# Decode step of two attention and two FFN layers on Trainium2: FFN products moved to other PSUM banks, and pauses between small steps

## The chip, the cores and the metric

The kernel runs on one core of one Trainium2 chip. The metric is the device time of one execution in microseconds (us). The time before is the median of three runs.

## The reference

One token per batch row (8 rows, width D = 640) goes through attention, FFN, attention, FFN. Both attention layers use the same cache of keys and values (32 heads, 4096 positions, 128 wide, in bfloat16) and the same weights; so do both FFNs.

```python
def _A_ref(x, k_cache, v_cache, wq, wo):
    q = (x @ wq).reshape(B, Sq, 32, 128).transpose(0, 2, 1, 3)
    scores = jnp.einsum("bhqd,bhkd->bhqk", q, k_cache) * (128 ** -0.5)
    p = _softmax(scores, axis=-1)
    o = jnp.einsum("bhqk,bhkd->bhqd", p, v_cache)
    return o.transpose(0, 2, 1, 3).reshape(B, Sq, 32 * 128) @ wo

def _B_ref(x, w1, w2):                      # 640 -> 1728 -> 640
    return jnp.maximum(x @ w1, 0) @ w2

x = A_x
x = x + _A_ref(_layernorm(x), A_k_cache, A_v_cache, A_wq, A_wo)
x = x + _B_ref(_layernorm(x), B_w1, B_w2)
x = x + _A_ref(_layernorm(x), A_k_cache, A_v_cache, A_wq, A_wo)
x = x + _B_ref(_layernorm(x), B_w1, B_w2)
```

## The kernel before

**Visits and units.** Work goes by visits. A visit is one pair of heads of one batch row in one layer; there are 2 x 8 x 16 = 256 of them, numbered 0 to 255. A visit has a K part (scores) and a V part (weighted values), and each part has four units of 512 KB, 128 partitions by 4 KB. K48.2 is unit 2 of the K part of visit 48. V parts run one visit behind K parts: K48, K49, V48, V49, K50 and so on. Units are loaded into an arena of 26 slots by DMAs from SyncE (SP, L637). A load takes one to eight units that lie together in memory, if so many neighbouring slots are free.

**Kept tiles.** Since both layers read the same cache, 21 units of each row stay in the arena from the first layer to the second, and three more are parked in PSUM (`stash`, `unstash`). When the first layer of a row ends, 21 slots are held and five are left.

**Turns.** Eight times, once for each row, the first layer of a row ends and its second layer begins. Between the two lie two visits of another layer or row (`AHEAD = 2`); in the second turn these are 48 and 49. In them the FFN of the row that has just ended is computed, then the new mean and variance, and the queries of the second layer. That is the chain that `finish(0, b)` gives: `up` (five groups of matmuls with w1, 15, 15, 15, 15 and 10 of them), `var` and `root` (the layer norm's scale, on GpSimd), `relu`, `down` (five groups of 14 matmuls with w2), `add`, `mean`, `center`, a query Q, `var2`, `root2`, a query Q. The second layer's last row ends with `finish(1, b)`, which does the same for all eight rows at once.

**Small steps of a visit.** After the scores, M1 (maximum, VectorE), T (transpose, PE), M2 (maximum, VectorE), B (broadcast, PE), E (on ScalarE: the negative maximum, then the exponentials), in most visits PT and PC (turn the probabilities), L (their sum, PE) and I (its reciprocal, VectorE); after the values OC (ScalarE empties o_ps), OG, O, W (product with wo) and Y. A query is Q (ten matmuls) and QC (a copy on ScalarE). In most visits ("moving") the cache streams through PE against four columns of weights (L695, L687); around a turn the cache is the weight and the query moves (L705).

**The order.** `plan()` writes out one list of operations for all engines, and that list is the order in which each engine executes. PE takes its instructions in that order. After every unit of products there is a gap. `step()` fills it: each waiting chain offers its next step with a weight (about its number of matmuls), and those are taken until CAP is reached. A step of weight 0 follows at once. `feed()` puts loads into the list when slots come free; it uses a rough clock for the size of a load, which the weights advance.

**PSUM.** Four names matter here. `o_ps` (one bank) takes the values' products, and at a turn the scores of the first of the two visits; `s_ps` (one bank) takes the scores; `small_ps` (one bank) takes nearly every small result, each in columns of its own; `stash_ps` parks units. The FFN's `up` and `down` of one row are in `small_ps` (`ffn_ps`), and the sum L is in `small_ps` (`lsum_ps`), or in `s_ps` (`lsum2_ps`) for both visits before a turn:

```python
lsum2_ps = s_ps[:, 4 * NJ : 6 * NJ]
mean2_ps, var2_ps, q2_ps = (s_ps[:, 6 * NJ + lo : 6 * NJ + hi] for lo, hi in ((0, 1), (1, 2), (2, 4)))
...
h = [ffn_ps[:, :FC].rearrange("p (f b) -> p f b", b=1)] * len(up_parts)
y = ffn_ps[:, FC * B : FC * B + DC].rearrange("p (c b) -> p c b", b=1)
```

Lines that the text names: L549 `up`, L580 `down`, L573 `relu`, L655 queries, L663 their copy, L680, L687 values, L695, L705 scores, L715 M1 at a turn, L739 B, L757 and L761 E, L781 L, L795 OC, L825 W.

Of the kernel before, what the change touches and what calls it, by code (L numbers as in the profile page):

```python
# [12 lines left out]
ALU = mybir.AluOpType  # L13
AX = mybir.AxisListType
# [8 lines left out]
SOON = 4  # L23
PACE, LATE = 0.6, 2
PAD = 2048
AHEAD = 2
BANK = 512
CAP = 20


def tile_at(NP, which, hp):
# [1 line left out]
    return max(0, 2 * hp - 1) if which == "K" else min(2 * hp + 2, 2 * NP - 1)  # L33


def plan(B, NP, n_up, n_down):

# [4 lines left out]
    order1 = list(range(NP - 1, NP - 4, -1)) + list(range(NP - 3))  # L44
    visits = [(0, 0, hp) for hp in order0]
# [11 lines left out]
    moving = [not any(t - AHEAD - 1 <= i < t + 5 for t in turns) and i < NV - 2 for i in range(NV)]  # L57
# [137 lines left out]
    def query(b, n):  # L195

        return [(10, ("Q", b, order1[n])), (0, ("QC", b, order1[n]))]
# [9 lines left out]
    def finish(layer, b):  # L207

        def own(n, *op):
            return n, ("C", layer, b, *op)  # L210

        c = []
        for k in range(n_up):
            c += [own(15, "up", k)]
            if layer:
                c += [own(0, "relu", k)]
            elif k == min(1, n_up - 1):
                c += [own(0, "var"), own(0, "root")]
        if layer:
            for k in range(n_up):  # L220
                c += [own(15, "down", k)] + [own(0, "var"), own(0, "root")] * (k == n_up // 2)
            return c + [own(0, "add")]
        c += [own(0, "relu")] + [own(14, "down", k) for k in range(n_down)] + [own(0, "add")]
        c += [own(2, "mean"), own(0, "center")] + query(b, 0)
        c += [own(1, "var2"), own(0, "root2")] + query(b, 1)
        return c

    feed()
    for which, i in slots:
        layer, b, hp = visits[i]  # L230
        if which == "K":
            if layer == 0 and b == 0 and hp % GP == 0:
                ops.append(("Q0", hp // GP))
                done.add(ops[-1])
            if layer:
                until(("QC", b, hp))
            if i + 2 < NV and visits[i + 2][0] and order1.index(visits[i + 2][2]) > 1:
                chains.append(query(visits[i + 2][1], order1.index(visits[i + 2][2])))
            pad(i)
            if i and (moving[i] or moving[i - 1]):  # L240
                until(("E", i - 1))
            if moving[i] and not moving[i - 1]:
                ops.append(("clear",))
        else:
            until(("PC" if moving[i] else "E", i))
            clock[0] = max(clock[0], ready.pop(i))
        for g in range(UNIT):
            u = find(which, i, g)
            ops.append(("mm", which, i, g, u))
            clock[0] = max(clock[0], lands[u]) + 0.5  # L250
            release(which, i, g)
            if g + 1 < UNIT:
                step()
        if which == "K":
            if layer and hp == order1[0]:
                until(("C", 0, b, "root2"))
            ops.append(("M1", i))
            ready[i] = clock[0] + 3
            step()
            turned = [(4, ("PT", i)), (0, ("PC", i))] if moving[i] else [(1, None)]  # L260
            chains.append([(1, ("T", i)), (0, ("M2", i)), (1, ("B", i)), (0, ("E", i))] + turned + [(1, ("L", i)), (0, ("I", i))])
        else:
            until(("I", i))
            if i + 1 < NV and moving[i + 1]:
                until(("PC", i + 1))
            if not direct[i]:
                ops.append(("OC", i))
                step()
                chains.append([(6, ("OG", i)), (0, ("O", i))])
            else:  # L270
                ops.append(("O", i))
                chains.append([])
            if i == NP - 2:
                ops.append(("WS", closing))
            if last_of[layer, b] == i and (layer == 0 or b == B - 1):
                chains[-1] += [(14, ("W", i)), (0, ("YC", i))] + finish(layer, b)
            elif layer == 0 or b == B - 1:
                chains[-1] += [(10, ("W", i)), (0, ("Y", i))]
                if last_of[layer, b] == next(v for v in range(i + 1, NV) if visits[v][:2] == (layer, b)):
                    chains[-1] += [(0, ("S", i)), (2, ("SM", i)), (0, ("SC", i))]  # L280
# [16 lines left out]
def kernel(  # L297
# [114 lines left out]
    turn_ps, max_ps, q1_ps = small_ps[:2, 80 : 80 + P], small_ps[:, 208:210], small_ps[:, 212:216]  # L412
    lsum_ps, ffn_ps, row_ps = small_ps[:, 216 : 216 + 2 * NJ], small_ps[:, 280:440], small_ps[:, 280 : 280 + P]
    P_ps = small_ps[:, 440 : 440 + 2 * NJ]
    lsum2_ps = s_ps[:, 4 * NJ : 6 * NJ]
    mean2_ps, var2_ps, q2_ps = (s_ps[:, 6 * NJ + lo : 6 * NJ + hi] for lo, hi in ((0, 1), (1, 2), (2, 4)))
    o2_ps = o_ps[:, :1], s_ps[:, 8 * NJ - 1 : 8 * NJ]
    per = GW // (2 * BANK)
    stash_ps = ps.tile([P, (STASH * per - 1) * 2 * BANK], BF16, name="stash_ps")
# [1 line left out]
    assert len(stash) > DC  # L421
    nc.vector.memset(o_ps, 0.0)

    up_parts = [range(f, min(f + 3, FC)) for f in range(0, FC, 3)]
    visits, moving, direct, ahead, ops = plan(B, NP, len(up_parts), DC)
    s_tiles, P_rows, P_tiles, m_tiles, o_tiles, oy, invL, oT, nmax, st = ({} for _ in range(10))

    def first_norm(xln):
# [61 lines left out]
    def over_partitions(out, t):  # L490
        for k in range(2):
            nc.tensor.matmul(out, lhsT=ones_p, rhs=t[:, :, k], start=(k == 0), stop=(k == 1))
# [38 lines left out]
    def finish_steps(layer, b):  # L531
# [2 lines left out]


        b0, nb = (b, 1) if layer == 0 else (0, B)
        x = xT[:, b0 : b0 + nb, :]
        if layer:
            h = [(ffn_ps if k % 2 else s_ps)[:, : FC * nb].rearrange("p (f b) -> p f b", b=nb) for k in range(len(up_parts))]
            y = stash_ps.bitcast(FP32).rearrange("p (c n) -> p c n", n=BANK)[:, :DC, :nb]  # L540
        else:
            h = [ffn_ps[:, :FC].rearrange("p (f b) -> p f b", b=1)] * len(up_parts)
            y = ffn_ps[:, FC * B : FC * B + DC].rearrange("p (c b) -> p c b", b=1)

        def up(k):
            for f in up_parts[k]:
# [7 lines left out]
        def var():  # L554
            over_partitions(var_ps[:, :nb], st.pop("s2"))

        def var2():
            over_partitions(var2_ps, st.pop("s2"))

        def root():  # L560
            if layer:
                st["rstd"] = root_of_all(var_ps[:, :nb])
# [4 lines left out]
        def relu(k=None):  # L567
            if not k:
                st["hT"] = temp([P, nb, FC], BF16, "hT").rearrange("p b f -> p f b")
            part = range(FC) if k is None else up_parts[k]  # L570
            for rows, lo, hi in ((P, part[0], min(part[-1] + 1, n_full)), (Dff % P, n_full, part[-1] + 1)):
                if rows and lo < hi:
                    nc.vector.tensor_scalar(  # L573
                        out=st["hT"][:rows, lo:hi], in0=h[k or 0][:rows, lo:hi], scalar1=0.0, scalar2=None, op0=ALU.max
                    )

        def down(k):
            for c, f in [(k, f) for f in range(FC)] if layer == 0 else [(c, f) for f in up_parts[k] for c in range(DC)]:
                fs = f_sizes[f]
                nc.tensor.matmul(  # L580
                    y[:, c, :], lhsT=w2_sb[:fs, f, c * P : (c + 1) * P], rhs=st["hT"][:fs, f, :],
                    start=(f == 0), stop=(f == FC - 1),
                )
# [24 lines left out]

        def root2():
            r = q_scale[b] = sm.tile([P, 2], FP32, name="q_scale", bufs=2)  # L610
            inverse_root(r[:, 0:1], var2_ps, float(Dh))
            nc.gpsimd.tensor_scalar(out=r[:, 1:2], in0=r[:, 0:1], scalar1=-1.0, scalar2=None, op0=ALU.mult)

        return dict(up=up, var=var, root=root, relu=relu, down=down, add=add, mean=mean, center=center, var2=var2, root2=root2)

    xlns, q_scale, finishing = {}, {}, {}

# [30 lines left out]
        nc.scalar.copy(out=qo[:, :, g * 2 * GP : (g + 1) * 2 * GP], in_=q_ps.rearrange("p h b -> p b h"))  # L648

    def do_q(b, hp):  # L650
        q_ps = st["q", b, hp] = q2_ps if hp == NP - 1 else q1_ps[:, 2 * (hp % 2) : 2 * (hp % 2) + 2]
        g, n = divmod(hp, GP)
        for h in range(2):
            for c in range(DC):
                nc.tensor.matmul(  # L655
                    q_ps[:, h : h + 1], lhsT=wq_sb[:, g, c, (2 * n + h) * Dh : (2 * n + h + 1) * Dh],
                    rhs=xlns[b][:, 0, c : c + 1], start=(c == 0), stop=(c == DC - 1),
                )
# [120 lines left out]

    def do_l(i):  # L780
        nc.tensor.matmul(  # L781
            lsum2_ps if ahead[i] else lsum_ps, lhsT=ones_p, rhs=P_tiles[i].rearrange("p h j -> p (h j)"), start=True, stop=True
        )

    def do_i(i):
        L = sm.tile([P, 2], FP32, name="lsum")
        nc.vector.tensor_reduce(  # L787
            out=L, in_=(lsum2_ps if ahead[i] else lsum_ps).rearrange("p (h j) -> p h j", h=2), axis=AX.X, op=ALU.add
        )
        invL[i] = sm.tile([P, 2], FP32, name="invL", bufs=3)  # L790
        nc.vector.reciprocal(out=invL[i], in_=L)
# [125 lines left out]
```

## Time and profile before

| | |
|---|---|
| median of 3 runs | 2341.08 us (2338.69 to 2342.32) |
| the profiled execution | 2344.78 us; its span, first to last instruction, 2343.0 us |
| DMA | 990.87 MB, mean 423 GB/s |
| loads of the cache | 521 DMAs of 512 to 4096 KB; 218 of them of 512 KB |
| PE busy | 1398.6 us (60%) |
| VectorE, ScalarE busy | 496.7 us (21%), 426.3 us (18%) |

In the profile PE is the matmul row and PEld the weight load, which overlaps it; DVE is VectorE, ACT ScalarE, POOL GpSimd and SP SyncE. A row of the timeline has the start in us, the time in us, engine, line, operation, output and input, how many, and in brackets how long the engine had been idle before and what released it. A row of the windows has the busy time of each engine in that stretch, then the granted PE clock, the DMA share and the GB/s moved.

### The profile page before, as it was taken

The page shows a single profiled execution, that of the slowest core. Times are in us where ns is not written, and L with a number is a line of the kernel's source. Part 1 is how long each engine was busy: PE and PEld are TensorE (multiplying, and loading weights), DVE is VectorE, ACT ScalarE, POOL GpSimd, SP SyncE. Part 2 cuts the span into 40 slices and gives each one's busy share as a digit, 9 for nine tenths or more (in the row PEclk, how much of TensorE's full clock was granted, in tenths as well). Part 3 has the DMA queues.
Part 4 walks back from the last instruction along what each step waited for, and adds up shares of the span by engine and source line. Part 5 has one row for each costly group of instructions (what it writes and reads, how often), then busy time and mean ns, then how long its engine had stood idle before and what let it go on. Part 6 is the DMA issues. An engine that isn't in the chain of part 4 may idle for free.

```text
span 2343.0 us, 43024 instructions
## 1 busy us (share of the span) xinstructions
PE 1398.6 (60%) x18748; PEld 591.4 (25%) x18748; DVE 496.7 (21%) x2022; ACT 426.3 (18%) x986; POOL 59.5 (3%) x296
## 2 busy tenths in 40 slices
PE   3547654576545764557545675556755567545766
PEld 1214211152111511125111241113411133111523
DVE  1113211131112211122111221112211122111312
ACT  1111211122111221112211121111211112111211
POOL 0000000000000000000000000000000000000000
PEclk9999999999999998555555555555555555555555
DMA  9999999999999999999999999999999999999997
GB/s 411 430 433 401 433 432 432 431 396 432 432 432 430 404 434 431 430 427 403 433 432 431 426 412 434 430 432 420 427 431 427 432 416 430 431 431 431 396 433 329
DMA packets 76753, 990.87 MB, mean 423 GB/s; under 512 B 8596, under 2 KB 8596, under 8 KB 36500
## 3 DMA queue, kind: packets, MB, share of 16 engines
q1 hardware_dynamic: 76564, 988.12, 99.4%
q8 instruction: 146, 2.39, 0.4%
q14 instruction: 43, 0.35, 0.0%
HBM read 988.08 MB, written 0.01 MB: 422 GB/s over the span
## 4 chain that ended last, share of the span: by engine, by line
DMA 71%; PE 17%; ACT 6%; DVE 3%; issue 2%; SPq 0%; POOL 0%; ACTq 0%; DVEq 0%; POOLq 0%
DMA arena<-in_A_kv_dram 71%; PE o_ps L687 5%; PE s_ps L695 4%; PE s_ps L705 2%; ACT P_row L755 2%; ACT o_sb L795 1%; PE small_ps L655 1%; DVE mrow L713 1%; ACT P_sb L761 1%; PE small_ps L800 1%; ACT arena L634 1%; PE small_ps L768 1%; PE small_ps L825 1%; DVE hmx L732 0%; ACT nmax L753 0%
## 5 line engine op out<-in xcount | busy, mean ns | idle before, releaser
L687 PE MATMUL o_ps<-arena,P_sb 128*4 128x512 bf16 x3952 | 584.3, 596 | 402.0 <-DMA arena<-in_A_kv_dram 401.0
L695 PE MATMUL s_ps<-arena,qz 128*4 128x512 bf16 x3040 | 410.3, 602 | 261.1 <-DMA arena<-in_A_kv_dram 249.5
L687 PEld LDWEIGHTS <-P_sb 128*4 128x4 bf16 x3952 | 107.4, 88 | 502.8 <-issue 491.7
L713 DVE TENSOR_REDUCE mrow<-s_ps 100x1 bf16<-100x512 f32 x190 | 131.8, 694 | 323.2 <-PE s_ps L695 323.2
L795 ACT CAST o_sb<-o_ps 100x512 bf16<-100x512 f32 x247 | 144.9, 587 | 289.3 <-PE o_ps L687 286.0
L753 ACT ACTIVATE nmax<-small_ps 100x1 f32<-100x1 f32 x106 | 18.1, 171 | 774.5 <-PE small_ps L742 774.5
L775 DVE CAST P_sb<-small_ps 128x64 bf16<-128x64 f32 x190 | 42.6, 224 | 523.1 <-PE small_ps L768 523.1
L695 PEld LDWEIGHTS <-qz 128*4 128x4 bf16 x3040 | 63.9, 85 | 313.7 <-issue 295.5
L705 PEld LDWEIGHTS <-arena 128*128 128x128 bf16 x4224 | 129.6, 104 | 40.8 <-DMA arena<-in_A_kv_dram 23.4
L705 PE MATMUL s_ps<-qo,arena 128*128 128x1 bf16 x3712 | 123.7, 165 | 17.2 <-ACT P_sb L761 7.6
L768 PE MATMUL small_ps<-few,P_row 100*128 100x16 bf16 x760 | 52.3, 179 | 92.1 <-ACT P_row L755 92.1
L753 ACT ACTIVATE nmax<-small_ps,q_scale 100x1 f32<-100x1 f32 x84 | 22.0, 261 | 398.7 <-PE small_ps L742 398.7
L787 DVE TENSOR_REDUCE lsum<-small_ps 128x2 f32<-128x64 f32 x240 | 53.9, 224 | 171.9 <-PE small_ps L781 171.9
L768 PEld LDWEIGHTS <-P_row 100*128 100x128 bf16 x760 | 35.0, 107 | 186.5 <-ACT P_row L755 178.2
L720 PE MATMUL small_ps<-few,mrow 100*1 100x16 bf16 x190 | 34.4, 181 | 67.6 <-DVE mrow L713 67.6
L755 ACT ACTIVATE P_row<-s_ps,nmax 100x512 bf16<-100x512 f32 x106 | 72.8, 687 | 3.4
L800 PEld LDWEIGHTS <-o_sb 100*128 100x128 bf16 x988 | 45.7, 106 | 107.2 <-ACT o_sb L795 73.8
L655 PE MATMUL small_ps<-xq,wq_sb 128*128 128x1 bf16 x1200 | 48.8, 165 | 38.9 <-DVE qo L812 33.5
L800 PE MATMUL small_ps<-few,o_sb 100*128 100x2 bf16 x988 | 65.1, 170 | 10.7 <-DVE lsum L787 2.2
L727 DVE TENSOR_REDUCE diag<-small_ps 1x2 bf16<-1x16 f32 x190 | 30.8, 162 | 186.9 <-PE small_ps L720 186.9
L720 PEld LDWEIGHTS <-mrow 100*1 100x1 bf16 x190 | 15.0, 79 | 210.8 <-DVE mrow L713 210.8
L755 ACT ACTIVATE P_row<-s_ps,nmax,q_scale 100x512 bf16<-100x512 f32 x84 | 65.3, 778 | 2.8
(225 smaller groups left out, 958.0 us busy)
## 6 DMA issues: line engine op xcount, KB each, us to landing
arena<-in_A_kv_dram SPq DMA_DIRECT2D x124, 4096.0 KB, 23.1
arena<-in_A_kv_dram SPq DMA_DIRECT2D x98, 2048.0 KB, 22.7
arena<-in_A_kv_dram SPq DMA_DIRECT2D x218, 512.0 KB, 6.5
arena<-in_A_kv_dram SPq DMA_DIRECT2D x48, 1024.0 KB, 11.3
arena<-in_A_kv_dram SPq DMA_DIRECT2D x11, 3072.0 KB, 22.4
arena<-in_A_kv_dram SPq DMA_DIRECT2D x11, 2560.0 KB, 20.5
arena<-in_A_kv_dram SPq DMA_DIRECT2D x10, 1536.0 KB, 19.7
wq_sb<-in_A_wq_dram SPq DMA_DIRECT2D x4, 1280.0 KB, 17.6
```

Source lines behind the costliest of these rows:

```text
L655: nc.tensor.matmul(q_ps[:, h : h + 1], lhsT=wq_sb[:, g, c, (2 * n + h) * Dh : (2 * n + h + 1) * Dh], rhs=xlns[b][:, 0, c : c + 1], start=( ...
L687: nc.tensor.matmul(o_ps[32 * c : 32 * c + CJ, :], lhsT=P_tiles[i][:, h, j : j + CJ], rhs=arena[:, at + c * CJ * Dh : at + (c + 1) * CJ * D ...
L695: nc.tensor.matmul(s_ps[32 * c : 32 * c + CJ, :], lhsT=qz[:, i % 3, c // 2, 3 - g : 3 - g + CJ], rhs=arena[:, at + c * BANK : at + (c + 1) ...
L705: nc.tensor.matmul(s_tiles[i][:, j : j + 1], lhsT=arena[:, at + n * P : at + (n + 1) * P], rhs=qo[:, b, h : h + 1], start=True, stop=True,)
L713: nc.vector.tensor_reduce(out=m_tiles[i][:OR, :1], in_=s_ps[:OR], axis=AX.X, op=ALU.max)
L720: nc.tensor.matmul(turn_ps[:1, : 4 * CJ], lhsT=m[:OR, :1], rhs=rsel[:OR], start=True, stop=True)
L755: nc.scalar.activation(out=P_rows[i][:OR], in_=s_ps[:OR], func=ACT.Exp, bias=nm[:OR, :1], scale=more)
L768: nc.tensor.matmul(P_ps[:, k * 4 * CJ : (k + 1) * 4 * CJ], lhsT=P_row[:OR, k * P : (k + 1) * P], rhs=rsel[:OR], start=True, stop=True,)
L775: nc.vector.tensor_copy(out=P_tiles[i].rearrange("p h (c k) -> p h c k", k=BANK // P), in_=P_ps.rearrange("p (k h c) -> p h c k", k=BANK / ...
L787: nc.vector.tensor_reduce(out=L, in_=(lsum2_ps if ahead[i] else lsum_ps).rearrange("p (h j) -> p h j", h=2), axis=AX.X, op=ALU.add)
L795: nc.scalar.copy(out=o_tiles[i][:OR], in_=o_ps[:OR, :].rearrange("p (j d) -> p j d", j=CJ))
L800: nc.tensor.matmul(oy[i][:, :2], lhsT=o_tiles[i][:OR, j, :], rhs=gsel[:OR, j, :], start=(j == 0), stop=(j == CJ - 1))
```

## The change

The order in which the cache's tiles are visited is the same. What changes:

- Of one row's FFN, `up` goes to columns of `o_ps` and `down` to columns of `s_ps`. `mean2` stays in `s_ps`; the second variance goes to `var_ps` in `small_ps`, where the first one is; the query of the last pair of heads goes to `small_ps` like the others. L of the visit two before a turn stays in `s_ps`, L of the visit one before goes to `small_ps`.
- The groups of `up` and `down` are counted in the plan (`UPS` = 3 blocks of w1, `DOWNS` = 1 column block), with their true weights. For one row `var` and `root` follow the first group of `up`, not the second. `relu` of one row is one instruction over all 14 blocks.
- Pauses, steps with no operation and weight 1: one after `add`, two ahead of the query of each later visit, and three or four (not one) ahead of L in the two visits before a turn, where L's weight is 3.
- CAP goes from 20 to 34.

```diff
+UPS, DOWNS = 3, 1
+LAST = 3
-CAP = 20
+CAP = 34
...
         c = []
-        for k in range(n_up):
-            c += [own(15, "up", k)]
-            if layer:
-                c += [own(0, "relu", k)]
-            elif k == min(1, n_up - 1):
-                c += [own(0, "var"), own(0, "root")]
         if layer:
-            for k in range(n_up):
-                c += [own(15, "down", k)] + [own(0, "var"), own(0, "root")] * (k == n_up // 2)
+            n = -(-n_f // LAST)
+            for k in range(n):
+                c += [own(15, "up", k), own(0, "relu", k)]
+            for k in range(n):
+                c += [own(15, "down", k)] + [own(0, "var"), own(0, "root")] * (k == n // 2)
             return c + [own(0, "add")]
-        c += [own(0, "relu")] + [own(14, "down", k) for k in range(n_down)] + [own(0, "add")]
-        c += [own(2, "mean"), own(0, "center")] + query(b, 0)
+        for f in range(0, n_f, UPS):
+            c += [own(n_c * min(UPS, n_f - f), "up", f // UPS)] + [own(0, "var"), own(0, "root")] * (f == 0)
+        c += [own(0, "relu")]
+        for k in range(0, n_c, DOWNS):
+            c += [own(n_f * min(DOWNS, n_c - k), "down", k // DOWNS)]
+        c += [own(0, "add"), (1, None), own(2, "mean"), own(0, "center")] + query(b, 0)
...
-                chains.append(query(visits[i + 2][1], order1.index(visits[i + 2][2])))
+                chains.append([(1, None)] * 2 + query(visits[i + 2][1], order1.index(visits[i + 2][2])))
...
-            turned = [(4, ("PT", i)), (0, ("PC", i))] if moving[i] else [(1, None)]
-            chains.append([(1, ("T", i)), (0, ("M2", i)), (1, ("B", i)), (0, ("E", i))] + turned + [(1, ("L", i)), (0, ("I", i))])
+            turned = [(4, ("PT", i)), (0, ("PC", i))] if moving[i] else [(1, None)] * (5 - ahead[i] if ahead[i] else 1)
+            chains.append([(1, ("T", i)), (0, ("M2", i)), (1, ("B", i)), (0, ("E", i))] + turned + [(3 if ahead[i] else 1, ("L", i)), (0, ("I", i))])
...
-    lsum2_ps = s_ps[:, 4 * NJ : 6 * NJ]
-    mean2_ps, var2_ps, q2_ps = (s_ps[:, 6 * NJ + lo : 6 * NJ + hi] for lo, hi in ((0, 1), (1, 2), (2, 4)))
+    up_ps, down_ps, mean2_ps = o_ps[:, 4 * NJ : 4 * NJ + FC], s_ps[:, 4 * NJ : 4 * NJ + DC], s_ps[:, 5 * NJ : 5 * NJ + 1]
+    lsum2_ps = s_ps[:, 5 * NJ + 8 : 7 * NJ + 8]
...
-            h = [ffn_ps[:, :FC].rearrange("p (f b) -> p f b", b=1)] * len(up_parts)
-            y = ffn_ps[:, FC * B : FC * B + DC].rearrange("p (c b) -> p c b", b=1)
+            h = [up_ps.rearrange("p (f b) -> p f b", b=1)] * len(up_parts)
+            y = down_ps.rearrange("p (c b) -> p c b", b=1)
...
-            for rows, lo, hi in ((P, part[0], min(part[-1] + 1, n_full)), (Dff % P, n_full, part[-1] + 1)):
+            whole = FC if k is None else n_full
+            for rows, lo, hi in ((P, part[0], min(part[-1] + 1, whole)), (Dff % P, whole, part[-1] + 1)):
...
-        q_ps = st["q", b, hp] = q2_ps if hp == NP - 1 else q1_ps[:, 2 * (hp % 2) : 2 * (hp % 2) + 2]
+        q_ps = st["q", b, hp] = q1_ps[:, 2 * (hp % 2) : 2 * (hp % 2) + 2]
...
-            lsum2_ps if ahead[i] else lsum_ps, lhsT=ones_p, rhs=P_tiles[i].rearrange("p h j -> p (h j)"), start=True, stop=True
+            lsum2_ps if ahead[i] == AHEAD else lsum_ps, lhsT=ones_p, rhs=P_tiles[i].rearrange("p h j -> p (h j)"), start=True, stop=True
```

In the second turn the list of `plan()` then runs as follows (each line: the unit, then what is done in the gap after it, loads left out).

```
before                                         after
K48.1 up.0                                     up.0 var root
K48.2 up.1 var root                            up.1
K48.3 M1.48 up.2                               M1.48 up.2
K49.0 up.3 T.48 M2.48                          up.3 T.48 M2.48
K49.1 B.48 E.48 up.4 relu                      B.48 E.48 up.4 relu
K49.2 down.0                                   down.0
K49.3 M1.49 down.1 L.48 I.48                   M1.49 down.1
V48.0 down.2 T.49 M2.49                        down.2 T.49 M2.49
V48.1 down.3 B.49 E.49                         down.3 B.49 E.49 L.48 I.48
V48.2 down.4 add                               down.4 add
V48.3 OC.48 L.49 I.49 mean center              OC.48
V49.0 OG.48 O.48 Q15 QC                        mean center OG.48 O.48
V49.1 var2 root2 W.48 Y.48                     Q15 QC W.48 Y.48
V49.2 Q14 QC                                   var2 root2 L.49 I.49
V49.3 OC.49                                    OC.49 Q14 QC
K50.0 OG.49 O.49 Q13 QC                        OG.49 O.49
K50.1 W.49 Y.49                                W.49 Y.49
K50.2                                          Q13 QC
```

More of the change, by code (lines that the diff above doesn't have):

```diff
@@ L25, with plan @@
 PAD = 2048
+UPS, DOWNS = 3, 1
+LAST = 3
 AHEAD = 2
 BANK = 512
-CAP = 20
+CAP = 34
 def tile_at(NP, which, hp):
     return max(0, 2 * hp - 1) if which == "K" else min(2 * hp + 2, 2 * NP - 1)
-def plan(B, NP, n_up, n_down):
+def plan(B, NP, n_f, n_c):
     order0 = list(range(NP))
@@ L422 @@
     nc.vector.memset(o_ps, 0.0)
-    up_parts = [range(f, min(f + 3, FC)) for f in range(0, FC, 3)]
-    visits, moving, direct, ahead, ops = plan(B, NP, len(up_parts), DC)
+    visits, moving, direct, ahead, ops = plan(B, NP, FC, DC)
     s_tiles, P_rows, P_tiles, m_tiles, o_tiles, oy, invL, oT, nmax, st = ({} for _ in range(10))
@@ L536, in finish_steps @@
         b0, nb = (b, 1) if layer == 0 else (0, B)
+        n = LAST if layer else UPS
+        up_parts = [range(f, min(f + n, FC)) for f in range(0, FC, n)]
         x = xT[:, b0 : b0 + nb, :]
@@ L555, in var @@
             over_partitions(var_ps[:, :nb], st.pop("s2"))
-        def var2():
-            over_partitions(var2_ps, st.pop("s2"))
         def root():
@@ L577, in down @@
         def down(k):
-            for c, f in [(k, f) for f in range(FC)] if layer == 0 else [(c, f) for f in up_parts[k] for c in range(DC)]:
+            cs = range(k * DOWNS, min((k + 1) * DOWNS, DC))
+            for c, f in [(c, f) for c in cs for f in range(FC)] if layer == 0 else [(c, f) for f in up_parts[k] for c in range(DC)]:
                 fs = f_sizes[f]
@@ L610, in root2 @@
             r = q_scale[b] = sm.tile([P, 2], FP32, name="q_scale", bufs=2)
-            inverse_root(r[:, 0:1], var2_ps, float(Dh))
+            inverse_root(r[:, 0:1], var_ps[:, :1], float(Dh))
             nc.gpsimd.tensor_scalar(out=r[:, 1:2], in0=r[:, 0:1], scalar1=-1.0, scalar2=None, op0=ALU.mult)
-        return dict(up=up, var=var, root=root, relu=relu, down=down, add=add, mean=mean, center=center, var2=var2, root2=root2)
+        return dict(up=up, var=var, root=root, relu=relu, down=down, add=add, mean=mean, center=center, var2=var, root2=root2)
     xlns, q_scale, finishing = {}, {}, {}
@@ L787, in do_i @@
         nc.vector.tensor_reduce(
-            out=L, in_=(lsum2_ps if ahead[i] else lsum_ps).rearrange("p (h j) -> p h j", h=2), axis=AX.X, op=ALU.add
+            out=L, in_=(lsum2_ps if ahead[i] == AHEAD else lsum_ps).rearrange("p (h j) -> p h j", h=2), axis=AX.X, op=ALU.add
         )
```

## The prediction

> **What bounds the kernel now.** I read the page first: the DMA row, the bytes and the chain of waits.
>
> ```profile
> span 2343.0 us, 43024 instructions
> PE 1398.6 (60%) x18748; PEld 591.4 (25%) x18748; DVE 496.7 (21%) x2022; ACT 426.3 (18%) x986; POOL 59.5 (3%) x296
> ...
> DMA  9999999999999999999999999999999999999997
> GB/s 411 430 433 401 433 432 432 431 396 432 432 432 430 404 434 431 430 427 403 433 432 431 426 412 434 430 432 420 427 431 427 432 416 430 431 431 431 396 433 329
> ...
> q8 instruction: 146, 2.39, 0.4%
> ...
> DMA 71%; PE 17%; ACT 6%; DVE 3%; issue 2%; SPq 0%; POOL 0%; ACTq 0%; DVEq 0%; POOLq 0%
> ```
>
> All 40 slices but the last are full of DMA, and good ones move 432 GB/s. The 988.1 MB at 432 GB/s take 2287 us; the span is 56 us longer. The low slices (401, 396, 404, 403, 412, 416, 396) are the turns, where one batch row's FFN runs. PE at 60% is no bound on average, so an edit counts only where it starves the DMA. I therefore took windows of 10 us across the second turn and, after it, a quiet stretch; the last number is GB/s, the one before it the DMA share.
>
> ```profile
> 480.00:490.00 10.00, 7.76 (x214) 6.22 (x211) 3.19 (x20) 1.22 (x4) 0.56 (x3) 1.00 0.94 363
> 490.00:500.00 10.00, 8.15 (x177) 6.17 (x175) 1.71 (x10) 1.28 (x6) 1.78 (x8) 1.00 1.00 373
> 500.00:510.00 10.00, 8.07 (x173) 5.52 (x171) 2.82 (x18) 1.65 (x5) 2.54 (x12) 1.00 1.01 376
> 510.00:520.00 10.00, 8.09 (x174) 5.23 (x171) 2.36 (x12) 2.73 (x9) 0.00 (x0) 1.00 1.03 426
> 560.00:570.00 10.00, 5.70 (x62) 1.86 (x59) 1.76 (x7) 1.98 (x5) 0.00 (x0) 1.00 0.99 424
> ```
>
> Only 480 to 510 us falls short, by (69 + 59 + 56) / 432 x 10 = 4.3 us. The reason is in `plan`: 21 of 26 arena slots hold kept tiles there, five are left, and for 16 units of 512 KB in a row (K48 to V49; both kernels) the loads run just four units ahead. A slot goes round as landing, products, release, next load. In the DMA view 17 loads of that stretch need 5.5 to 7.5 us from issue to landing, median 5.6. Five slots in 5.6 + 0.6 us of products give 1.24 us a unit; landings in fact come every 1.25 us. So whatever delays PE between a landing and the end of that unit's products comes close to delaying the DMA. The timeline there shows who waits:
>
> ```profile
> 489.79 0.23 DVE L715 TENSOR_REDUCE mrow<-o_ps 128x2 bf16<-128x64 f32 x1 [0.55 <-PE o_ps L705]
> ...
> 490.43 0.59 PE L705 MATMUL s_ps<-qo,arena 128*128 128x1 bf16 x16 [0.28 <-DMA arena<-in_A_kv_dram]
> ...
> 492.18 0.18 PE L739 MATMUL small_ps<-diag,few 2*128 2x2 bf16 x1
> ...
> 492.60 0.47 ACT L761 ACTIVATE P_sb<-o_ps,nmax 128x32 bf16<-128x32 f32 x2
> 492.62 0.63 PE L549 MATMUL small_ps<-xf,w_sb 128*128 128x1 bf16 x10 [0.26 <-ACT nmax L757]
> ...
> 498.00 0.60 PE L687 MATMUL o_ps<-arena,P_sb 128*4 128x512 bf16 x4 [1.25 <-DMA arena<-in_A_kv_dram]
> ```
>
> PE waits 2.9 us for landings in this turn (485.3 to 506): that is its spare time. At 492.62 it waits for ScalarE's read of the score maximum, in other columns of the same bank.
>
> [...]
>
> **The change, part by part** (per turn; durations from the turn above).
> 1. `up` into o_ps. Those columns share a bank with the scores of visit 48. up(2) is queued behind M1 of K48.3: it began at 489.61, now it waits for the reduction to end at 490.02, **+0.45**. up(4) waited for the maximum only; now for the exponentials out of o_ps, which end at 493.07: **+0.50**. Behind it on PE are K49.2's products, whose slot SP waits to refill.
> 2. `down` into s_ps. down(1) is queued behind M1 of K49.3, which reads that bank from 494.80 for 0.23; it began at 494.62, now not before 495.07: **+0.45**.
> 3. L of visit 48 moves, by its weight of 3 and the pauses, from before V48.0 to just behind B of visit 49 and ahead of V48.2, and it writes s_ps, which E of visit 49 is reading. B ended at 499.26, both exponentials end at 499.98, then 0.2 for L: V48.2 starts at 500.20, not 499.23, **+0.97**; its old place gives back 0.2.
> 4. After V48.3: `mean` and L of visit 49 used to run while ScalarE emptied o_ps (0.59, L795) and so cost nothing; that cover is gone. mean adds 0.2; L adds 0.23 and 0.27 waiting for DVE's read of `var`, now in its bank: **+0.7**. Query 15 now lies in small_ps, so W of visit 48 behind it waits for ScalarE's copy: **+0.25**.
> 5. Given back: the queries of heads 13, 0, 1 no longer stand behind the O they waited for (0.32, 0.37 and more, L655), but from K50 on, where loads run 5 to 13 units ahead. Worth **-0.8** of PE, almost nothing of DMA. One relu instruction less: 0.1 of DVE, hidden.
> 6. CAP, groups of three, LAST = 3, `whole`: no change in instructions or bytes; the last row's finish has the same PE order. 0.
> 7. SP: the planner's clock shifts, so 503 loads instead of 521, same 1856 units. The least lead outside turns that falls is 21 to 11 units, 13 us of transfers against landings of 5 to 7 us. 0. POOL has the same instructions; root2 starts about a unit later, M1 of K50 is 5 us away. 0.
>
> Sum: 0.45 + 0.50 + 0.45 + 0.77 + 0.7 + 0.25 = **3.1 us of PE more** before K50, against 2.9 us of spare waits. Followed unit by unit: K49.2 is 0.6 late, V48.0 0.8, V48.1 not at all (its landing is later still), V48.2 0.95, V49.0 0.8, V49.2 1.15. What the DMA loses is lateness less the slack of a load. The shortest landing seen in a turn is 4.9 us (first turn), in others 5.3 to 5.5; the medians are 5.6 to 6.0. So the slack is 0.1 to 1.1, and 1.15 late costs 0.05 to 1.05; I take 0.6. Eight turns: **4.8 us**. Unknown is the wait on the bank: no less than zero if the moved steps' readers finish before PE arrives, at most the 0.72 us from B to the end of the exponentials, in items 1 and 3.
>
> The profiled execution took 2344.78 us; the sum makes it about 2349.6. It is 3.7 above the median of the runs, 2341.08, so I carry the difference: 2346.
>
> **Rivals.** (a) Forecast: new bank waits in the closed loop, 0.3 to 1.1 a turn, 2343.5 to 2350, centre 2346. For it: the loop's margin of 0.01 to 0.6 us. (b) *Not slower*: [...] PE's 2.9 us of spare hide it all, and early queries release K50's slots sooner. Decisive if the median landing stays above 4.9 + 1.15 = 6.05 us at 1.15 late. It gives 2341; with the starvation of before cured as well [...] 2338. Against: medians of 5.6 to 6.0. (c) PE becomes the bound: beyond 1.25 us a unit lateness is never made up and all 3.1 less 0.8 us reach the end, 8 x 2.3 = 18: 2359. [...] (d) It doesn't do what it says, since the moved products keep the engines apart no better: the reads at once are only exchanged for others, and with equal waits 2341.
>
> **Numbers.** (a) 0.52, (b) 0.27, (c) 0.11, (d) 0.10. A measurement can tell 0.2% (4.7 us) from no change. Slower by more: half of (a), (c) and what lies between them, 0.48. Within: the other half of (a), most of (b), (d), 0.43. Faster by more needs all starvation cured and more, 0.09. Range 2338 to 2357; (a) alone 2343.5 to 2350.
>
> **What would show it.** Right: in a turn, up(2), up(4) and L wait for DVE or ACT readers of o_ps and s_ps for 0.4 to 0.7 us; V48.2 comes about 1 us later behind B; GB/s of the three windows falls to about 350 to 370; landings in the turn get shorter (5.0 to 5.3) [...]. Wrong: landing times stay and the span does too (b), or PE's waits for DMA vanish and unit steps exceed 1.3 us (c), or the quiet slices fall below 430, which would point to the loads of item 7.

## The result, and the profile after

The changed kernel takes **2347.56 us** (median of 6 runs, 2346.82 to 2347.88), the kernel before 2341.42 us beside it. The ratio is 1.0027, 95% interval 1.0014 to 1.0040: **slower by 6.3 us** (3.3 to 9.4), where 2346 was predicted (against 2341.08).

The page of the kernel after (first rows, busy time, slices, instruction queue, chain):

```profile
span 2345.0 us, 42966 instructions
PE 1394.8 (59%) x18748; PEld 580.1 (25%) x18748; DVE 496.6 (21%) x2014; ACT 425.5 (18%) x986; POOL 59.5 (3%) x296
...
GB/s 410 429 432 398 433 433 432 430 395 432 433 432 428 406 433 431 433 425 408 432 433 431 423 408 434 431 432 418 419 431 432 432 412 422 433 430 431 394 432 335
...
q8 instruction: 146, 2.39, 0.4%
...
DMA 36%; PE 11%; ACT 3%; DVE 2%; issue 1%; ACTq 0%; DVEq 0%; SPq 0%
```

No engine works longer, and the instruction queue (q8) has as many packets (146). Most quiet slices still move 430 to 434 GB/s; what differs is again in the low ones. The chain gives the DMA 36% where it gave 71%, but its shares now sum to half of the span, so I conclude nothing from it.

The spans of the two profiles differ by 2.0 us, the medians by 6.1. The profiled execution of before was 3.4 us above its median, that of after 0.7 below. So a single trace of each kernel can mislead by more than half of this change, and I set each against its own median below.

Windows of the kernel after over the second turn and a quiet stretch (the last number is GB/s):

```profile
480.00:490.00 10.00, 7.62 (x223) 6.62 (x220) 3.21 (x20) 0.59 (x1) 1.87 (x9) 1.00 1.01 395
490.00:500.00 10.00, 7.42 (x155) 5.46 (x152) 1.57 (x8) 1.28 (x6) 0.46 (x2) 1.00 1.01 389
500.00:510.00 10.00, 7.94 (x175) 5.32 (x172) 2.97 (x19) 1.55 (x5) 2.54 (x12) 1.00 0.94 325
...
560.00:570.00 10.00, 6.71 (x76) 2.05 (x79) 1.64 (x6) 1.79 (x4) 0.00 (x0) 1.00 1.01 434
```

The first three lose (37 + 43 + 107) / 432 x 10 = 4.3 us, as before. **One turn does not show this change.** The eight together do. I laid windows of 40 us over each turn, from 192, 478, 764, 1051, 1337, 1624, 1910 and 2196 us. Two of them, first of the kernel before, then of the kernel after:

```profile
478.00:518.00 40.00, 31.92 (x701) 22.82 (x702) 10.31 (x60) 6.86 (x24) 4.87 (x23) 1.00 0.99 384
...
1910.00:1950.00 40.00, 32.26 (x722) 23.35 (x721) 10.18 (x60) 6.88 (x24) 4.87 (x23) 0.50 1.01 405
```

```profile
478.00:518.00 40.00, 31.52 (x707) 22.38 (x704) 10.22 (x59) 6.62 (x23) 4.87 (x23) 1.00 0.99 381
...
1910.00:1950.00 40.00, 32.23 (x722) 22.95 (x723) 10.34 (x59) 6.62 (x23) 4.86 (x23) 0.50 1.00 393
```

The means of the eight are 396.75 and 391.0 GB/s, so the turns lose (432 - 396.75) x 320 / 432 = 26.1 us before and 30.4 after (six of the eight read lower, one the same, one higher). That is 4.3 us more, where the spans differ by 2.0: the whole loss of the change is in the turns. Set to the medians (26.1 - 3.4, 30.4 + 0.7) it is 22.7 and 31.1, 8.4 more where the medians differ by 6.1. This takes what a profiled execution is off its median as lying in the turns, which is not shown.

The timeline of the kernel after, PE, ScalarE and VectorE in the second turn (start, time, engine, line, operation; in brackets the idle time and its end):

```profile
489.00 0.23 DVE L718 TENSOR_REDUCE mrow<-o_ps 128x2 bf16<-128x64 f32 x1 [1.59 <-PE o_ps L708]
489.27 0.54 PE L553 MATMUL o_ps<-xf,w_sb 128*128 128x1 bf16 x15 [0.32 <-DVE mrow L718]
...
491.79 0.47 ACT L764 ACTIVATE P_sb<-o_ps,nmax 128x32 bf16<-128x32 f32 x2
492.31 0.63 PE L553 MATMUL o_ps<-xf,w_sb 128*128 128x1 bf16 x10 [0.76 <-ACT P_sb L764]
...
494.75 0.60 PE L583 MATMUL s_ps<-hT,w_sb 128*128 128x1 bf16 x14 [0.31 <-DVE mrow L718]
...
498.45 0.18 PE L742 MATMUL small_ps<-diag,few 2*128 2x2 bf16 x1
...
499.39 0.21 PE L784 MATMUL s_ps<-P_sb,few 128*128 128x64 bf16 x1 [0.76 <-ACT P_sb L764]
...
499.54 0.60 PE L690 MATMUL o_ps<-arena,P_sb 128*4 128x512 bf16 x4
...
501.90 0.59 PE L690 MATMUL o_ps<-arena,P_sb 128*4 128x512 bf16 x4 [0.69 <-ACT o_sb L798]
```

The kernel before, at the same places:

```profile
489.61 0.54 PE L549 MATMUL small_ps<-xf,w_sb 128*128 128x1 bf16 x15
...
494.62 0.60 PE L580 MATMUL small_ps<-hT,w_sb 128*128 128x1 bf16 x14
...
499.08 0.18 PE L739 MATMUL small_ps<-diag,few 2*128 2x2 bf16 x1
499.23 0.59 PE L687 MATMUL o_ps<-arena,P_sb 128*4 128x512 bf16 x4
...
501.74 0.59 PE L687 MATMUL o_ps<-arena,P_sb 128*4 128x512 bf16 x4
```

The changed kernel has five waits for readers of a bank: up(2) behind M1 (L718), up(4) behind the exponentials, down(1) behind M1, L behind the exponentials, and V49.0 behind ScalarE's emptying of o_ps. The first four are for readers of other columns; V49.0 overwrites the very columns that are read, and before, that wait was covered by other work. V48.2 (499.54) comes 1.09 us behind B (498.45); before it came 0.15 behind (499.23 after 499.08).

### The profile page after: what moved, and what is told of

Read it like the earlier page. It is cut to its first block, busy times and chain, and to the rows that moved or that the text cites. A ratio compares the mean times of both kernels' runs of the same rounds, so it can differ in the third digit from the quotient of the medians.

```text
span 2345.0 us, 42966 instructions
## 1 busy us (share of the span) xinstructions
PE 1394.8 (59%) x18748; PEld 580.1 (25%) x18748; DVE 496.6 (21%) x2014; ACT 425.5 (18%) x986; POOL 59.5 (3%) x296
## 4 chain that ended last, share of the span: by engine, by line
DMA 36%; PE 11%; ACT 3%; DVE 2%; issue 1%; ACTq 0%; DVEq 0%; SPq 0%
DMA arena<-in_A_kv_dram 36%; PE o_ps L690 3%; PE s_ps L698 3%; PE s_ps L708 2%; ACT P_row L758 1%; DVE mrow L716 1%; ACT P_sb L764 1%; PE small_ps L658 1%; ACT arena L637 1%; ACT o_sb L798 1%; PE small_ps L803 0%; PE s_ps L583 0%; PE small_ps L828 0%; PE small_ps L771 0%; ACT nmax L760 0%
## 5 line engine op out<-in xcount | busy, mean ns | idle before, releaser
L698 PE MATMUL s_ps<-arena,qz 128*4 128x512 bf16 x3040 | 416.4, 595 | 338.7 <-DMA arena<-in_A_kv_dram 327.3
L690 PEld LDWEIGHTS <-P_sb 128*4 128x4 bf16 x3952 | 101.8, 85 | 435.8 <-issue 420.6
L708 PE MATMUL s_ps<-qo,arena 128*128 128x1 bf16 x3712 | 128.8, 165 | 15.2 <-ACT P_sb L764 7.6
L756 ACT ACTIVATE nmax<-small_ps,q_scale 100x1 f32<-100x1 f32 x84 | 21.9, 261 | 292.0 <-PE small_ps L745 292.0
L658 PEld LDWEIGHTS <-wq_sb 128*128 128x128 bf16 x1280 | 45.4, 105 | 71.7 <-issue 71.5
## 6 DMA issues: line engine op xcount, KB each, us to landing
arena<-in_A_kv_dram SPq DMA_DIRECT2D x72, 2048.0 KB, 20.7
```

The lines of the kernel that those rows point to most:

```text
L658: nc.tensor.matmul(q_ps[:, h : h + 1], lhsT=wq_sb[:, g, c, (2 * n + h) * Dh : (2 * n + h + 1) * Dh], rhs=xlns[b][:, 0, c : c + 1], start=( ...
L690: nc.tensor.matmul(o_ps[32 * c : 32 * c + CJ, :], lhsT=P_tiles[i][:, h, j : j + CJ], rhs=arena[:, at + c * CJ * Dh : at + (c + 1) * CJ * D ...
L698: nc.tensor.matmul(s_ps[32 * c : 32 * c + CJ, :], lhsT=qz[:, i % 3, c // 2, 3 - g : 3 - g + CJ], rhs=arena[:, at + c * BANK : at + (c + 1) ...
L708: nc.tensor.matmul(s_tiles[i][:, j : j + 1], lhsT=arena[:, at + n * P : at + (n + 1) * P], rhs=qo[:, b, h : h + 1], start=True, stop=True,)
```

## The experiments

Each value "over before" is the ratio less 1, times 2341 us, with its 95% interval. "PE's own time" is read off the timeline: from the start of K48.0 to that of K50.0 (and the like in other turns), less PE's waits for a DMA in between and less waits that nothing in the profile ends (see experiment 6), as a mean over the first seven turns of the trace; PE's waits for other engines count in it. At 432 GB/s the 16 units land in 16 x 524,288 / 432,000 = 19.4 us, an estimate from what the quiet slices move; own time beyond that is more than the DMA needs. "Loss" is that of the eight windows, set to the kernel's median as above.

| kernel | slots | over before, us | PE's own time, us | loss in turns, us |
|---|---|---|---|---|
| before | 5 | 0 | 17.6 | 22.7 |
| **after** | 5 | 6.3 (3.3 to 9.4) | 20.7 | 31.1 |
| banks alone | 5 | 2.8 (1.2 to 4.2) | 18.6 | 24.6 |
| order alone | 5 | 3.7 (1.9 to 5.6) | 19.1 | 27.7 |
| after, L as before | 5 | 3.5 (1.9 to 5.2) | 19.4 | 27.6 |
| after, L and banks as before | 5 | -1.4 (-3.5 to 0.5) | 17.7 | 21.9 |
| before, FFN first in a gap | 5 | -0.7 (-2.8 to 1.2) | 17.8 | 23.9 |
| both of the last two | 5 | -1.4 (-3.3 to 0.5) | 17.7 | 21.1 |
| before, down(3) three times | 5 | 7.7 (4.9 to 10.8) | 18.4 | 31.8 |
| before | 6 | 3.5 (2.1 to 5.2) | 17.5 | 17.0 |
| before, down(3) three times | 6 | 5.4 (3.3 to 7.5) | 18.4 | 20.4 |
| after, L and banks as before | 6 | 4.4 (2.8 to 5.9) | 17.9 | 18.5 |
| after, L as before | 6 | 6.6 (4.0 to 9.4) | 20.0 | 21.6 |
| after | 6 | 9.6 (6.6 to 12.4) | 21.0 | 25.8 |

A sixth slot keeps one tile less per row: 4.19 MB more to load, 9.7 us at 432 GB/s. Less those 9.7 us, the differences of time follow the differences of the last column within about 3 us in every row. Without setting anything to a median: the span of the profiled execution, less its own loss in the turns and less the 9.7 us where there are six slots, is 2313 to 2317 us in all fourteen traces, while the spans range from 2337 to 2347 us. So all of these kernels differ in the turns and hardly elsewhere.

The expectations weigh three theories: the closed loop (a late PE makes a late load), banks alone (the moved products are the whole cause), and loads (the other sizes of the loads are).

**1. Banks alone.** The kernel before with `up` in o_ps and `down` in s_ps; its order is untouched.

```diff
-            h = [ffn_ps[:, :FC].rearrange(...)] * len(up_parts)
-            y = ffn_ps[:, FC * B : FC * B + DC].rearrange(...)
+            h = [o_ps[:, 4 * NJ : 4 * NJ + FC].rearrange(...)] * len(up_parts)
+            y = s_ps[:, 6 * NJ + 8 : 6 * NJ + 8 + DC].rearrange(...)
```

> The kernel before with its own order, but with one row's up in o_ps and down in s_ps (the banks of the change). Loop theory (a PE that is late in the 16 units with four loads ahead delays the DMA): PE waits 0.3 behind M1.48, 0.76 behind E.48 and 0.3 behind M1.49, so it is 0.6 to 0.8 us late from K49.2 to V48.0, where loads still have slack; 0.1 to 0.3 us a turn, +1 to +2 us. Banks alone (the moved products are the whole cause): +6. Loads (the cause is that the planner's clock issues other sizes): 0, since the loads are those of before.

2.8 us, a little over what the theory of the closed loop gave, and short of the 6 of banks alone. The waits of up(2), up(4) and down(1) are there in its trace with 0.32, 0.76 and 0.32 us.

**2. Order alone.** The changed kernel with its results in the banks of before; order, pauses and CAP as changed.

```diff
-    up_ps, down_ps, mean2_ps = o_ps[...], s_ps[...], s_ps[:, 5 * NJ : 5 * NJ + 1]
+    lsum2_ps = s_ps[:, 4 * NJ : 6 * NJ]
+    mean2_ps, var2_ps, q2_ps = (s_ps[:, 6 * NJ + lo : 6 * NJ + hi] for lo, hi in ((0, 1), (1, 2), (2, 4)))
+    up_ps, down_ps = ffn_ps[:, :FC], ffn_ps[:, FC * B : FC * B + DC]
...
```

> The changed order, pauses, weights and CAP, but every small result in the bank where it was before. Loop theory: L of visit 48 behind B of visit 49 still waits 0.76 for the exponentials, L.49 still behind var2; V48.2 to V49.3 0.8 late, +3 to +5. Banks alone: 0. Loads: +6, since the loads are those of the change.

3.7 us: the pauses cost something without any move of banks, as expected. L's wait is here too, 0.76 us.

**3. After, L as before.** Only L's pause and weight undone.

```diff
-turned = ... else [(1, None)] * (5 - ahead[i] if ahead[i] else 1)
-... [(3 if ahead[i] else 1, ("L", i)), (0, ("I", i))]
+turned = ... else [(1, None)]
+... [(1, ("L", i)), (0, ("I", i))]
```

> The changed kernel with the old pause and weight of L, so that L.48 is issued behind down.1 and L.49 behind OC.48 again. Loop theory: the wait of 0.76 in front of V48.2 is gone, the waits behind M1 and E.48 stay; +1 to +3 against before. Banks alone: +6. Loads: +6 if the loads change little against the changed kernel.

3.5 us: a little above the range, but about half is gone.

**4. L and banks as before.** Experiments 2 and 3 together: what is left of the change is the order of the FFN, the pauses ahead of the queries, and CAP.

> The changed order with L's pause and weight as before, and all results in the banks of before: what is left of the change is var after the first group, mean after V49.0, the pauses ahead of queries, one relu, and the loads. Loop theory: mean, Q and W stand later, about 0.3 us late at V49.1 and V49.2, within the slack: 0 to +1.5. Loads: +3 to +6.

-1.4 us, not told apart from the kernel before. So the **whole loss lies in L's place and the banks**, and the rest of the change, its fewer loads included (502 here, 503 in the changed kernel, 521 before), costs 0.5 us at most by the interval. The changed kernel and experiments 2, 3 and 4 form a square: the banks cost 4.9 us with L as before and 2.6 with L moved; L costs 5.1 alone and 2.8 on top of the banks; together they cost 7.7, less than the 10 of their sum, though with intervals of some 2 us each the difference is not certain. "Banks" in this square takes in the banks of the second variance, of the last query and of L of the later visit; experiment 1 left these alone, so its 2.8 is not the same quantity as the 4.9. The waits of experiment 4 in 483 to 504 us of the second turn (us in total, times, longest):

```profile
PE o_ps L712 <- DMA arena<-in_A_kv_dram: 1.5, 3, 1.0
PE o_ps L694 <- DMA arena<-in_A_kv_dram: 1.2, 3, 0.5
PE o_ps L694 <- ACT o_sb L802: 0.5, 1, 0.5
PE small_ps L554 <- ACT nmax L764: 0.3, 1, 0.3
PE s_ps L712 <- DMA arena<-in_A_kv_dram: 0.2, 1, 0.2
```

PE waits for DMAs again (2.9 us), and for readers only twice.

**5. A delay without a wait.** The kernel before, with down(3), between V48.1 and V48.2, done three times; its sums stay as they are. I put that at 1.24 us of PE per turn at one place, twice the 0.62 of one group.

```diff
-for c, f in [(k, f) for f in range(FC)] if layer == 0 else
+for c, f in [(k, f) for f in range(FC)] * (1 + 2 * (k == 3)) if layer == 0 else
```

> The kernel before, with the 14 products of down.3 of one row issued three times (the first start again from zero, so the sums are the same): 1.24 us of PE between V48.1 and V48.2, no new wait, same loads. Loop theory: about as late as L makes it in the changed kernel; (1.24 less a slack of 0.4 to 0.7) x 7 or 8 turns, +4 to +7. If PE's spare time hides lateness: 0 to +1. Banks alone and loads: 0.

7.7 us (7.5 between the medians), a little above the range of the closed loop (4 to 7). The 42 products take 1.73 us where 14 took 0.62, so the delay is 1.11 us rather than 1.24, and it costs 0.96 a turn. PE still waits 1.9 us a turn for landings. The timeline of that kernel shows why this is no cover:

```profile
495.42 0.60 PE L687 MATMUL o_ps<-arena,P_sb 128*4 128x512 bf16 x4 [1.52 <-DMA arena<-in_A_kv_dram]
...
497.18 1.73 PE L580 MATMUL small_ps<-hT,w_sb 128*128 128x1 bf16 x42
...
498.95 0.60 PE L687 MATMUL o_ps<-arena,P_sb 128*4 128x512 bf16 x4
```

The wait (1.52, at V48.0) comes *ahead* of the delay. Here the spare time that lay before the delay did not absorb it. The products of V48.2, which free its slot, start 2.29 us behind those of V48.1 (498.95 after 496.66) where it was 1.23 in the kernel before (499.23 after 498.00). That the load released by that slot starts late is inferred; experiment 7 bears it out (1.9 us with a sixth slot where it is 7.7 with five).

**6. A sixth slot.** If lateness counts only through a late slot, one more slot should hide it.

```diff
-SPARE = 5
+SPARE = 6
```

The kernel after:

> The changed kernel with SPARE = 6: 20 units of a row are kept, not 21, so one unit more is loaded for each row (8 x 1.21 = +9.7 us of transfers) and six slots go round at a turn instead of five: 1.2 us more slack. Loop theory: the change's extra lateness (up to 1.15 us) is covered, so this is within 0 to 2 us of the kernel before with SPARE = 6, not 6 away from it; against the kernel before +5 to +9. If the 6 us come from elsewhere than the five-slot loop: the difference between the two stays 6.

The kernel before:

> The kernel before with SPARE = 6: +9.7 us of transfers, less what starvation at turns there is in the kernel before (about 0.4 us a turn, 3 us): +5 to +9 on the loop theory. If nothing starves in the kernel before: +9.7.

Here **the expectation fell**. Before with six slots is 3.5 us slower, not 5 to 9: of the 9.7 us of bytes, 6.2 come back from less starvation. After with six is 9.6 slower: there 6.4 come back (9.7 less 9.6 - 6.3). So the sixth slot helps both alike, and the distance between the two is 6.1 us, as large as with five. The waits of PE in the second turn show the reason. After, six slots, 485 to 507 us:

```profile
PE s_ps L784 <- ACT P_sb L764: 0.8, 1, 0.8
PE o_ps L553 <- ACT P_sb L764: 0.8, 1, 0.8
PE o_ps L690 <- ACT o_sb L798: 0.7, 1, 0.7
PE small_ps L658 <- DVE oT L815: 0.4, 1, 0.4
PE s_ps L583 <- DVE mrow L718: 0.3, 1, 0.3
PE o_ps L553 <- DVE mrow L718: 0.3, 1, 0.3
PE small_ps L784 <- DVE root L463: 0.2, 1, 0.2
PE small_ps L828 <- ACT qo L666: 0.2, 1, 0.2
PE small_ps L494 <- DVE s2h L488: 0.2, 1, 0.2
```

Before, six slots, 485 to 505 us:

```profile
PE o_ps L687 <- DMA arena<-in_A_kv_dram: 1.0, 3, 0.7
PE small_ps L549 <- ACT nmax L757: 0.4, 1, 0.4
PE s_ps L492 <- DVE lsum L787: 0.3, 1, 0.3
PE s_ps L705 <- DMA arena<-in_A_kv_dram: 0.2, 1, 0.2
PE o_ps L705 <- DMA arena<-in_A_kv_dram: 0.2, 1, 0.2
```

With the change there is no wait for a DMA left in this turn (0.2 us a turn over the seven): the units are there when PE comes, and PE's own time, 21.0 us, is beyond the 19.4 us of the DMA. Then PE is the slower one in these units, and a sixth slot does not bring the two kernels closer.

The six-slot traces show one more thing. PE stopped, mostly in the middle of a group whose data had landed, and nothing in the profile ends the wait. Of the kernel before with six slots:

```profile
1926.60 0.48 PE L705 MATMUL s_ps<-qo,arena 128*128 128x1 bf16 x12
1927.83 0.25 PE L705 MATMUL s_ps<-qo,arena 128*128 128x1 bf16 x4 [0.75 <-issue]
```

That trace has nine such waits of over 0.15 us, 6.9 us in all; the changed kernel with six slots has five (2.6 us), before and after with five slots none. What ended them, no run shows.

**7. Does the sixth slot hide a plain delay?** Experiment 5 again, with six slots.

> The kernel before with the down product of the fourth column three times per turn (its sums left as they are), now with six free arena slots. With five slots that 1.24 us of TensorE work at one place, ahead of the value products that free load 2.19, cost 7.5 us, though TensorE still waited some 2 us a turn for landings. If it cost that much because a late slot makes a late load, the sixth slot hides it: 3 to 5 us over the kernel before with five slots, that is 0 to 2 us over the kernel before with six (3.1). If TensorE's time in the 16 units costs whatever the slots, as with the changed kernel's waits at six slots, it stays 5 to 8 us over that: 8 to 11 us over the kernel before.

5.4 us, that is 1.9 over the kernel before with six: within the range of the late slot. The same delay that cost 7.7 us with five slots loses three quarters of that, though each of these numbers is uncertain by 2 to 3 us. PE's own time (18.4) stays under 19.4 here. So the sixth slot tells **two mechanisms** apart: late slots, which it hides, and PE's own time beyond the DMA's, which it does not. That PE's own time is what makes the difference is read from the table, not set by an experiment of its own.

**8. Which part of the change is which?** With six slots, L as before, and then L and banks as before.

> The changed kernel with six free arena slots, and with the row-sum product L paused one gap and weighing 1, as in the kernel before; all else as changed. With six slots the kernel before took 3.1 us more than with five, the changed one 9.0 us more. If what is left of the change at six slots is TensorE's own time in the 16 units behind the loads (no wait for a DMA in them), taking L's 0.97 us and what follows it out of each turn must give most of it back: 3.5 to 6.5 us over the kernel before with five slots. If instead the sixth slot brings a loss of its own that the order of L does not touch, it stays at 8 to 10 us. If only the loads' lateness counted, a sixth slot would have hidden L's wait already and nothing changes: 8.5 to 9.5 us.

> The changed kernel's order of gaps and pauses with six free arena slots, L as before, and all small results in the banks that they had before (no product of the FFN behind a reader of its bank). If TensorE's own time is the whole cause, this stands where the kernel before with six slots stands, 1 to 4 us over the kernel before with five. If the order of the steps itself costs something apart from L and the banks, 5 to 8 us.

6.6 and 4.4 us. The first is just above its range (3.5 to 6.5) and below those of the other theories; L is worth 3.0 us of the 9.6. The second is just above its range (1 to 4), below that of the other theory (5 to 8), and within 1 us of the kernel before with six (3.5). In the order of PE's own time (17.5, 17.9, 18.4, 20.0, 21.0) the six-slot kernels stand at 3.5, 4.4, 5.4, 6.6 and 9.6 us. L and banks cost 9.6 - 4.4 = 5.2 us with six slots and 7.7 with five. Taken at face value two thirds of the loss is PE's own time and one third late slots. But from the kernel before to the changed one, 6.1 of 6.3 us stay with six slots; with these intervals the split is open between two thirds and all.

**9. A version that beats both?** The kernel before, with the FFN's group ahead of the small steps in each gap and the pauses ahead of the queries; and the same key in the kernel of experiment 4.

```diff
-for c in sorted(now, key=lambda c: len(c) > 1 and not c[1][0]):
+for c in sorted(now, key=lambda c: (c[0][1] is None or c[0][1][0] != "C", len(c) > 1 and not c[1][0])):
...
-chains.append(query(...))
+chains.append([(1, None)] * 2 + query(...))
```

> The kernel before with the FFN's group ahead of the small steps in each gap (up.4 ahead of B.48, so that it no longer waits 0.26 us for ScalarE) and the pauses ahead of later queries: the attempt at a faster one. Loop theory: 0.3 us less of PE in K49, where loads have slack, and an earlier K50.1: -2 to 0. If PE time in the loop counts in full (0.8 us of the end per us, as tripled products suggest): -2. Loads: 505 instead of 521, +3 to +6 if their sizes were the cause.

> Five slots, the changed order with L as before and all small results in the banks of the kernel before, and in each gap the FFN's products ahead of the small steps. Either half alone was 1 to 2 us under the kernel before. If both take time of TensorE's own off the 16 units, this is 2 to 4 us faster than the kernel before and 8 to 10 us faster than the changed one; if they use the same spare time, 0 to 2 us faster than the kernel before.

-0.7 and -1.4 us: faster than the changed kernel by 7 to 8 us, but neither is told from the kernel before. The two gains don't add. The first has 505 loads for 521 and is not slower, which once more speaks against the loads.

## Why the prediction was right, and where it was not

**Right: the place and the sum.** The bank waits lie where items 1 to 4 put them, in the 16 units of each turn. Over the first seven turns PE's waits for other engines rise from 0.6 to 3.8 us a turn and its own time from 17.6 to 20.7: **3.1 us more**, the sum forecast. That it fits to a tenth is luck in part: the items below miss by 0.13 and 0.14 one way, and a wait of 0.55 that was not foreseen goes the other.

**Items 1 and 2.** up(4) waits 0.76 us where it waited 0.26: +0.50, as said. up(2) and down(1) wait 0.32 and 0.31 where +0.45 was said; the reader's own 0.23 and some 0.1 around it are all that is paid. In each of these waits the columns are disjoint. Each bank here is one tile of the program, so no run tells whether the wait follows the bank or the tile.

**Item 3.** V48.2 comes 1.09 us behind B where it came 0.15 behind: +0.94, where +0.97 was said.

**Item 4.** The wait of 0.69 for ScalarE's emptying of o_ps, once covered by `mean` and L.49, stands bare, and L.49 waits 0.25 for the root; W waits 0.25 for the query's copy. As said. Not foreseen: query 15 waits 0.55 for VectorE's copy of the O before it.

**Items 5 to 7.** Undoing L and banks alone brings the time back to that of before; so nothing else costs anything that can be measured here.

**The step that was wrong: "lateness less the slack of a load", with "2.9 us of spare waits" beside it.** It gave 0.6 us a turn; measured are 6.3 / 8 = 0.8 (0.4 to 1.2), so the total of 4.8 us was near by luck as much as by reason. It assumed that the DMA's turnaround of five slots was the only limit, so that a late unit lost a part once and then recovered. The spare waits do shrink, from 2.6 to 0.7 us a turn, but the 16 units get 1.2 us longer (20.2 to 21.4), that is 1.33 us a unit, and with six slots the loss stays. That was rival (c)'s mechanism and its sign (DMA waits that all but vanish, steps above 1.3 us); its price, 18 us, was not: about a third reached the end. Why no more than a third does, no run shows.

**Wrong: one size and one sign.** Landings were to get shorter, 5.0 to 5.3 us. In the second turn they stay at 5.6 (DMA view of the kernel after, 484 to 507 us: operation, count, size, median from issue to landing):

```profile
arena<-in_A_kv_dram SPq DMA_DIRECT2D x16, 512.0 KB, 5.6
```

Over the first seven turns the medians go from 5.6 to 6.2 us down to 5.4 to 5.6, so they do get shorter, by less than was said. And the three windows were to fall to 350 to 370 GB/s; they read 395, 389 and 325, with the same loss as before. A single turn's windows move as much from one late landing (6.8 us at 494 to 497 us of the kernel before, where 5.6 is the median) as from the change; only the eight turns together carry it.

## What to carry to other kernels

In a loop of loads, products and few free slots, ask two questions of a delay: does it hold up a slot whose load is on the critical path, and does the engine's own time, waits for its neighbours included, still fit into the transfers' time. An extra slot answered them apart here: it hid the first, not the second. And idle time of an engine that came ahead of the delay was no spare time here (experiment 5: a wait of 1.52 us in the second turn, and 0.96 us a turn lost all the same); and a small result is best left in a bank that no other engine reads at that moment, since PE waited here for readers of other columns too, 0.31 to 0.76 us each time.

## What the runs showed of the hardware

- The granted clock fell from 1.00 to 0.50 in the profiled executions before and after, at different times (mean 0.696 and 0.639), without a mark on these products: 16 of 128x128 against one column took 0.59 us at 485 us of the kernel before (clock 1.00) and 0.59 at 1632 us (clock 0.50). The down groups took 0.60 to 0.62 at both. Of the changed kernel, the execution whose mean clock was 1.00 took 2347.43 us and the one at 0.575 took 2347.69.
- In the second turn of the changed kernel PE stood idle for 0.31 and 0.32 us behind a VectorE reduction of 0.22 and 0.23 us out of the same bank, and twice for 0.76 us behind the negative maximum and the exponentials on ScalarE (0.17 + 0.47).
- With six slots PE stopped, mostly within groups of products whose data had landed: for 0.75 us at 1927.83 of the kernel before, nine times and 6.9 us in all in that trace, and for up to 1.56 us (at 204.45) in that of experiment 7. With five slots, where PE waited 2.9 us (before) and 1.4 us (after) for landings in the second turn, the kernels before and after had no such stop.
